# q times kᵀv for two heads: two 64-row halves of the TensorE array in place of one block-diagonal matrix

## The chip, the cores and the metric

The kernel runs on one core of a Trainium2 chip. The metric is device time of one execution in microseconds (us). A profiled execution has a span some 1.8 us shorter than its device time. A speed ratio is the mean time of one kernel's fast runs over the mean of the other's in the same rounds on the same chip, so it is not quite the ratio of the medians quoted beside it.

## The reference, cut to what matters

```python
def _attn_ref(q, k, v, g_norm):                      # 8 batches, 8 heads, 576 tokens, 64 wide, fp32
    kv = np.einsum('bhsd,bhse->bhde', k, v)
    out = np.einsum('bhsd,bhde->bhse', q, kv)
    rms = np.sqrt(np.mean(out * out, axis=-1, keepdims=True) + 1e-06)
    return (out / rms * g_norm).astype(np.float32)
def _moe_ref(x, w_gate, w_val, w_out):               # x: 4608 tokens x 512
    gate = 1.0 / (1.0 + np.exp(-(x @ w_gate)))
    val = x @ w_val
    return (gate * val @ w_out).astype(np.float32)
```

## The kernel before

Attention is done for two heads at a time, 32 pairs in all. A pair's work is a list of small steps. The first eight pairs are scheduled by hand at the start, while weights are still being converted on VectorE. The other 24 go, one step per "slot", between the matmuls of the feed-forward layers.

```python
    kvs = [const.tile([P, P], FP32, name=f"kv{i}") for i in range(2)]
    # ... zeroed once: the two off-diagonal blocks stay zero
        def kv_mm():                  # k^T v: head e on its half of the array's columns
            d["kv"] = ps = at_ps()
            for j in range(NJ):
                js = slice(HD * j, HD * j + HD)
                for e in range(2):
                    nc.tensor.matmul(ps[HD * e:HD * e + HD, 0, 0:HD], pairs[n]["k"][:, e, js], pairs[n]["v"][:, e, js],
                                     start=(j == 0), stop=(j == NJ - 1))
        def kv_out():                 # the two 64x64 blocks onto the diagonal
            for e in range(2):
                es = slice(HD * e, HD * e + HD)
                nc.vector.tensor_copy(out=kvs[n % 2][es, es], in_=d["kv"][es, 0, 0:HD])
            load_kv(n + 2)
        # ... q_mm, q_out: q is transposed, both heads' 64 rows on 128 partitions
        def u_mm():                   # q (k^T v): 96 tokens of both heads at a time
            ps = at_ps()
            d["u"] = ps[0:NP, :, 0:JH * P]
            for j in range(NJ):
                c0 = P * (j % JH)
                nc.tensor.matmul(ps[0:NP, j // JH, c0:c0 + P], d["qT"][:, j // JH, NP * (j % JH):NP * (j % JH) + NP],
                                 kvs[n % 2], start=True, stop=True)
        # ... u_square (ScalarE), u_sum (VectorE), u_root (ScalarE), u_norm (VectorE), x_mm (transposes), x_out
        return [kv_mm, kv_out, q_mm, q_out, u_mm, u_square, u_sum, u_root, u_norm, x_mm, x_out]
```

Here `P` is 128, `HD` 64, `NP` 96, `NJ` 6 and `JH` 3. After the first stage all attention steps share one PSUM tile of two banks ("at" in the profile); the first stage has four of them ("two").

## Time and profile before

| | before |
|---|---|
| time, median of 3 | 1215.44 us (1212.87 to 1215.98) |
| span of the profiled run | 1213.0 us |
| TensorE busy | 1172.0 us, 97% |
| VectorE busy | 473.5 us, 39% |
| to the second layer's first matmul | 220.6 us |
| from there to the first matmul of the fast first layer | 118.0 us |
| from there to the end | 874.4 us |

The last three rows cut the span at two landmarks of TensorE's own stream. The first stretch holds waits, in the other two TensorE is all but saturated. The second landmark can be read in the view of one line's instructions (first and last start are in us):

```profile
L489 PE MATMUL mm<-xT,gv x672: 379/379/483, 338.6 to 1160.2; 128*128 128x256 f32 x168
```

The first of these matmuls starts at 338.6 us, and 1213.0 - 338.6 = 874.4 us.

### The profile page before, as it was taken

The page shows a single profiled execution, that of the slowest core. Times are in us where ns is not written, and L with a number is a line of the kernel's source. Part 1 is how long each engine was busy: PE and PEld are TensorE (multiplying, and loading weights), DVE is VectorE, ACT ScalarE, POOL GpSimd, SP SyncE. Part 2 cuts the span into 40 slices and gives each one's busy share as a digit, 9 for nine tenths or more (in the row PEclk, how much of TensorE's full clock was granted, in tenths as well). Part 3 has the DMA queues.
Part 4 walks back from the last instruction along what each step waited for, and adds up shares of the span by engine and source line. Part 5 has one row for each costly group of instructions (what it writes and reads, how often), then busy time and mean ns, then how long its engine had stood idle before and what let it go on. Part 6 is the DMA issues. An engine that isn't in the chain of part 4 may idle for free.

```text
span 1213.0 us, 13391 instructions
## 1 busy us (share of the span) xinstructions
PE 1172.0 (97%) x5136; PEld 786.9 (65%) x5136; DVE 473.5 (39%) x845; ACT 308.5 (25%) x577; POOL 241.8 (20%) x342
## 2 busy tenths in 40 slices
PE   4788999999999999999999999999999999999998
PEld 4444444455478846885588648874888478748863
DVE  4667878303034412543045404540345125504430
ACT  3444121113033312431143203420334021101110
POOL 0000000100024401331044203330244015403410
PEclk9889999999999999999999999999999999999999
DMA  9544322131012101120211102110110000010000
GB/s 243 136 129 134 104 104 70 29 78 46 17 47 60 30 18 47 31 59 9 56 30 31 38 26 59 30 31 26 40 29 1 18 18 1 1 27 9 1 9 26
DMA packets 71582, 57.48 MB, mean 47 GB/s; under 512 B 40800, under 2 KB 65376, under 8 KB 71520
## 3 DMA queue, kind: packets, MB, share of 16 engines
q1 hardware_dynamic: 68992, 56.05, 17.0%
q10 hardware_dynamic: 2528, 0.59, 0.3%
q8 instruction: 41, 0.67, 0.2%
q14 instruction: 21, 0.17, 0.0%
HBM read 47.19 MB, written 9.44 MB: 47 GB/s over the span
## 4 chain that ended last, share of the span: by engine, by line
PE 93%; DVE 3%; ACT 2%; DMA 1%; issue 1%; ACTq 0%; SPq 0%; DVEq 0%
PE mm L489 42%; PE mm L321 23%; PE two L341 13%; PE two L321 7%; PE at L238 2%; PE two L238 2%; PE at L211 1%; PE at L264 1%; DVE sq L256 1%; PE at L224 1%; PE two L211 1%; DMA q<-in_q_dram 1%; ACT L251 1%; PE two L264 1%; DVE ms L247 1%; ACT sq L243 1%
## 5 line engine op out<-in xcount | busy, mean ns | idle before, releaser
L472 POOL TENSOR_TENSOR tw<-gv 128x256 f32<-128x256 f32 x168 | 120.4, 728 | 913.8 <-PE mm L489 691.5
L321 PE MATMUL mm<-wo,gv 128*128 128x512 f32 x672 | 290.5, 592 | 0.0
L489 PE MATMUL mm<-sx,tw 128*128 128x256 f32 x1008 | 234.2, 380 | 0.0
L321 PEld LDWEIGHTS mm<-wo,gv 128*128 128x128 f32 x672 | 127.3, 190 | 155.3 <-issue 155.0
L489 PEld LDWEIGHTS mm<-sx,tw 128*128 128x128 f32 x1008 | 188.8, 190 | 24.6
L341 PE MATMUL two<-xT,gv 128*128 128x512 f32 x384 | 176.7, 611 | 14.3 <-DVE gv L159 14.3
L501 DVE TENSOR_TENSOR gv<-mm,p 128x256 f32<-128x256 f32 x84 | 35.7, 425 | 321.2 <-PE mm L489 321.2
L489 PE MATMUL mm<-xT,gv 128*128 128x256 f32 x672 | 159.7, 380 | 1.2 <-ACT sg L326 1.2
L489 PEld LDWEIGHTS mm<-xT,gv 128*128 128x128 f32 x672 | 126.0, 190 | 21.2 <-issue 2.9
L341 PEld LDWEIGHTS two<-xT,gv 128*128 128x128 f32 x384 | 72.2, 195 | 98.2 <-issue 93.1
L472 POOL TENSOR_TENSOR tw<-gv,tw 128x256 f32<-128x256 f32 x168 | 126.2, 771 | 1.1
L321 PE MATMUL two<-wo,gv 128*128 128x512 f32 x192 | 84.6, 594 | 0.0
L326 ACT COPY sg<-mm 128x512 f32<-128x512 f32 x28 | 16.4, 585 | 264.5 <-PE mm L321 264.5
L510 DVE TENSOR_TENSOR gv<-mm,p 128x256 f32<-128x256 f32 x84 | 35.6, 424 | 114.3 <-PE mm L489 114.3
L489 PE MATMUL mm<-sx,gv 128*128 128x256 f32 x336 | 79.9, 381 | 0.0
L489 PE MATMUL mm<-xT,tw 128*128 128x256 f32 x336 | 79.9, 381 | 0.0
L519 ACT ACTIVATE sg<-sg 128x256 f32<-128x256 f32 x84 | 35.0, 417 | 162.9 <-DVE sg L518 161.6
L489 PEld LDWEIGHTS mm<-xT,tw 128*128 128x128 f32 x336 | 63.0, 190 | 8.5
L489 PEld LDWEIGHTS mm<-sx,gv 128*128 128x128 f32 x336 | 63.0, 190 | 8.5
L526 DVE TENSOR_TENSOR gv<-gv,sg 128x512 f32<-128x512 f32 x84 | 66.6, 832 | 0.2
L321 PEld LDWEIGHTS two<-wo,gv 128*128 128x128 f32 x192 | 35.8, 190 | 41.8 <-issue 41.6
L495 ACT COPY p<-mm 128x256 f32<-128x256 f32 x84 | 31.3, 372 | 93.5 <-PE mm L489 93.5
(67 smaller groups left out, 824.7 us busy)
## 6 DMA issues: line engine op xcount, KB each, us to landing
k<-in_k_dram SPq DMA_DIRECT2D x32, 288.0 KB, 3.5
v<-in_v_dram SPq DMA_DIRECT2D x32, 288.0 KB, 4.1
q<-in_q_dram SPq DMA_DIRECT2D x60, 144.0 KB, 3.1
st<-in_moe_w_gate_dram SPq DMA_DIRECT2D x12, 512.0 KB, 3.9
st<-in_moe_w_val_dram SPq DMA_DIRECT2D x12, 512.0 KB, 5.1
st<-in_moe_w_out_dram SPq DMA_DIRECT2D x12, 512.0 KB, 4.1
out_dram<-sg SPq DMA_DIRECT2D x24, 192.0 KB, 2.3
out_dram<-sg SPq DMA_DIRECT2D x24, 128.0 KB, 2.3
```

What stands on the lines that cost most here:

```text
L211: nc.tensor.matmul(ps[HD * e:HD * e + HD, 0, 0:HD], pairs[n]["k"][:, e, js], pairs[n]["v"][:, e, js], start=(j == 0), stop=(j == NJ - 1))
L238: nc.tensor.matmul(ps[0:NP, j // JH, c0:c0 + P], d["qT"][:, j // JH, NP * (j % JH):NP * (j % JH) + NP], kvs[n % 2], start=True, stop=True)
L264: nc.tensor.transpose(ps[:, j // JH, c0:c0 + NP], d["xn"][:, j // JH, P * (j % JH):P * (j % JH) + P], ident[0:NP, 0:NP])
L321: nc.tensor.matmul(ps[:, i], gv[c, f][:, ts], w["wo", f], start=(f == 0), stop=(f == NFT - 1))
L341: nc.tensor.matmul(self.ps[:, i], w[("wg", "wv")[i], self.f][:, m, :], xT[self.c][:, m, :], start=(m == 0), stop=(m == NMT - 1), skip_grou ...
L472: nc.gpsimd.tensor_tensor(out=tw[f, i], in0=b[in0], in1=b[in1] if isinstance(in1, tuple) else tw[f, in1], op=ALU.subtract)
L489: nc.tensor.matmul(ps, wt[:, m, :], xs[:, m, :], start=(new and m == 0), stop=(m == NK - 1), skip_group_check=True)
L495: nc.scalar.copy(out=d["p1"], in_=pa)
L501: tt(out=d["h"][:, h1], in0=pb, in1=d["p1"], op=ALU.add)
L510: tt(out=d["h"][:, h2], in0=pb, in1=d["p1"], op=ALU.add)
L519: nc.scalar.activation(out=d["sg"][:, h2], in_=d["sg"][:, h2], func=AF.Sigmoid)
L526: tt(out=d["h"], in0=d["h"], in1=d["sg"], op=ALU.mult)
```

## The change

Half of the block-diagonal matrix is zeros, and TensorE multiplies by them. The change gives each head its own 64 rows of the array, with a dense 64x64 kᵀv as the moving operand, and its own PSUM bank. Zeros are no longer streamed, the memsets go, and two copies of 64x64 become one of 128x64.

```diff
-    kvs = [const.tile([P, P], FP32, name=f"kv{i}") for i in range(2)]
+    kvs = [const.tile([P, HD], FP32, name=f"kv{i}") for i in range(2)]
-    for kv in kvs:
-        nc.vector.memset(kv, 0.0)
...
-            for e in range(2):
-                es = slice(HD * e, HD * e + HD)
-                nc.vector.tensor_copy(out=kvs[n % 2][es, es], in_=d["kv"][es, 0, 0:HD])
+            nc.vector.tensor_copy(out=kvs[n % 2], in_=d["kv"][:, 0, 0:HD])
...
-            d["u"] = ps[0:NP, :, 0:JH * P]
+            d["u"] = ps[0:NP, :, 0:NJ * HD]
             for j in range(NJ):
-                c0 = P * (j % JH)
-                nc.tensor.matmul(ps[0:NP, j // JH, c0:c0 + P], d["qT"][:, j // JH, NP * (j % JH):NP * (j % JH) + NP],
-                                 kvs[n % 2], start=True, stop=True)
+                for e in range(2):
+                    es = slice(HD * e, HD * e + HD)
+                    nc.tensor.matmul(ps[0:NP, e, HD * j:HD * j + HD],
+                                     d["qT"][es, j // JH, NP * (j % JH):NP * (j % JH) + NP], kvs[n % 2][es, :],
+                                     start=True, stop=True)
```

The square, sum and normalisation read the result by head instead of by slice, and the normalisation writes it back in the old order; the transposes after it are unchanged.

More of the change, by code (lines that the diff above doesn't have):

```diff
@@ L234, in u_mm @@
             ps = at_ps()
-            d["u"] = ps[0:NP, :, 0:JH * P]
+            d["u"] = ps[0:NP, :, 0:NJ * HD]
             for j in range(NJ):
-                c0 = P * (j % JH)
-                nc.tensor.matmul(ps[0:NP, j // JH, c0:c0 + P], d["qT"][:, j // JH, NP * (j % JH):NP * (j % JH) + NP],
-                                 kvs[n % 2], start=True, stop=True)
+                for e in range(2):
[3 more added lines that the diff above has]
+                                     start=True, stop=True)
         def u_square():
-            d["sq"] = sb.tile([NP, 2, JH * P], FP32, tag="sq", name="sq")
+            d["sq"] = sb.tile([NP, 2, NJ * HD], FP32, tag="sq", name="sq")
             nc.scalar.activation(out=d["sq"], in_=d["u"], func=AF.Square)
         def u_sum():
-            d["ms"] = sb.tile([NP, 2, 2 * JH], FP32, tag="ms", name="ms")
+            d["ms"] = sb.tile([NP, 2, NJ], FP32, tag="ms", name="ms")
             nc.vector.tensor_reduce(out=d["ms"].rearrange("p i n -> p (i n)"),
@@ L254, in u_norm @@
             nc.vector.reciprocal(d["ms"], d["ms"])
-            d["xn"] = d["sq"]
-            nc.vector.tensor_tensor(out=d["xn"].rearrange("p i (n d) -> p i n d", d=HD),
-                                    in0=d["u"].rearrange("p i (n d) -> p i n d", d=HD),
-                                    in1=d["ms"].unsqueeze(3).to_broadcast([NP, 2, 2 * JH, HD]), op=ALU.mult)
+            d["xn"] = d["sq"].rearrange("p e f -> p (e f)")
+            nc.vector.tensor_tensor(out=d["xn"].rearrange("p (j e d) -> p e j d", e=2, d=HD),
+                                    in0=d["u"].rearrange("p e (j d) -> p e j d", d=HD),
+                                    in1=d["ms"].unsqueeze(3).to_broadcast([NP, 2, NJ, HD]), op=ALU.mult)
         def x_mm():
@@ L263, in x_mm @@
                 c0 = NP * (j % JH)
-                nc.tensor.transpose(ps[:, j // JH, c0:c0 + NP], d["xn"][:, j // JH, P * (j % JH):P * (j % JH) + P],
+                nc.tensor.transpose(ps[:, j // JH, c0:c0 + NP], d["xn"][:, P * j:P * j + P],
                                     ident[0:NP, 0:NP])
```

## The prediction

> **What bounds the kernel now.** I read the page first, then the groups by line and shape, then the stretches, the chain of waits, and last the timeline of one attention pair record by record. The busy table says that TensorE is the bound:
>
> ```profile
> PE 1172.0 (97%) x5136; PEld 786.9 (65%) x5136; DVE 473.5 (39%) x845; ACT 308.5 (25%) x577; POOL 241.8 (20%) x342
> ```
>
> TensorE is busy 97% and nothing else passes 65%, so what matters is how long TensorE's own stream of matmuls takes. By stretches (columns: stretch, its length, busy time and count of PE, PEld, DVE, ACT, POOL, granted clock, DMA share, GB/s) that does not hold from the start:
>
> ```profile
> 0.00:60.00 60.00, 38.29 (x264) 27.40 (x265) 30.46 (x46) 22.57 (x36) 0.70 (x6) 0.91 0.80 191
> 60.00:120.00 60.00, 48.91 (x223) 25.91 (x222) 42.43 (x55) 26.75 (x39) 0.00 (x0) 0.89 0.44 129
> 340.00:945.00 605.00, 602.26 (x3031) 450.81 (x3030) 225.35 (x480) 181.32 (x355) 169.31 (x240) 1.00 0.13 35
> ```
>
> Until 120 us TensorE waits about a quarter of the time (60 - 38.29 and 60 - 48.91) inside a chain matmul, square, sum, root, normalise, transpose. From 340 to 945 us it waits 2.7 of 605 us: each nanosecond put into its stream is paid in full there, and a faster VectorE or ScalarE pays nothing.
>
> The change touches L238, q times k^T v, once per pair of heads, 32 pairs. The groups by shape:
>
> ```profile
> L238 PE MATMUL at<-kv,qT 128*96 128x128 f32 x240 | 29.5, 273 | 0.0
> L238 PE MATMUL two<-kv,qT 128*96 128x128 f32 x144 | 21.2, 307 | 0.0
> L211 PE MATMUL at<-v,k 96*64 96x64 f32 x480 | 18.4, 226 | 0.0
> ```
>
> Six matmuls a pair appear as 12 records (240 records over 20 pairs): an fp32 matmul is two passes, each with its own weight load. L211, k^T v, is the model for the changed line: it already runs two heads at once, each on a half of the array's columns. Their real pace is in the timeline (start, length, engine, line, shapes, count):
>
> ```profile
> 340.52 0.92 PE L211 MATMUL at<-v,k 96*64 96x64 f32 x24
> 341.37 1.99 PE L489 MATMUL mm<-sx,tw 128*128 128x256 f32 x8
> 343.20 1.89 PE L489 MATMUL mm<-xT,gv 128*128 128x256 f32 x8
> 344.93 0.66 PE L224 MATMUL at<-ident,q 96*128 96x96 f32 x6
> 345.42 3.65 PE L489 MATMUL mm<-sx,tw 128*128 128x256 f32 x16
> 348.91 1.47 PE L238 MATMUL at<-kv,qT 128*96 128x128 f32 x12
> 350.22 1.89 PE L489 MATMUL mm<-xT,tw 128*128 128x256 f32 x8
> ```
>
> Take starts, not lengths, since lengths overlap. From 348.91 to 350.22 the 12 passes of L238 hold TensorE 1.31 us, 109 ns each, with no gap before or after. A pass of L489 takes 216 ns ((344.93 - 343.20) / 8), so passes cost about 0.83 ns per column plus 2.5. L211's inner starts come in twos, 6 to 7 ns apart, one pair every 58 ns: two passes of 64 columns in the time of one (64 x 0.83 + 5), so the column halves do run together. But L211's block costs more than 12 x 58 = 0.70 us. The previous L489 pass starts at 340.21 and should have streamed until 340.43; L211's first weights are loaded only at 340.52 (0.09 lost); nothing runs ahead of that load, so it is exposed (about 0.05); after the last pass (start 341.21, streamed by 341.27) the next load is at 341.37 (0.10 lost), and that load of 128 columns is exposed too: the following eight records take 1.99 instead of 1.89 (0.10 lost). The sum is 0.70 + 0.34 = 1.04 us, and every L211 block from 340 us on has the same gaps to 1 ns. L238 and L224 have none of them. So using the array in halves has an entry and exit price of about a third of a microsecond.
>
> **What the Trainium skill says.** "TensorEngine Tiling (Array Packing)", Key Properties: changing the tiling mode drains TensorE, and different tiles can load and multiply in parallel. The trace agrees on both for column halves (0.34 us; starts 6 to 7 ns apart). "TensorE: Matmul & The Clock Gate", LDWEIGHTS: a load takes its columns over 1.2 GHz, whatever the contraction rows. The trace's single loads are 190, 163 and 138 ns for 128, 96 and 64 columns, a slope of 0.81 ns a column: it agrees, with some 85 ns of latency that overlaps. The same page, Part 3, What overlaps: loads and matmuls of different row groups overlap. No row-split matmul runs in the kernel before, so this trace cannot confirm it. The first page's Gotcha 1 wants row tiles in different PSUM banks; the change does that.
>
> **The change part by part.** The stationary operand stays a slice of qT, 96 columns, now twice with 64 rows each; the moving operand shrinks from 128 columns to 64. So 12 passes of (load 96, stream 128) become 24 of (load 96, stream 64), 12 on each half.
>
> A pass now streams for 64 x 0.83 = 53 ns, but the weights behind it need 96 x 0.83 = 80 ns, plus 2.5. Before, an 80 ns load hid under a 107 ns stream. Now it does not: a half has one load in flight beside its running pass, so it steps at about 85 ns (82.5 plus the 2.5 by which L211's 58 also exceeds 53 + 2.5). That a load longer than the pass above it is paid is seen after L224: its last transpose covers 82 ns of a 128-column load of 110 ns, and the 16 records after it take 3.65 us against 16 x 0.216 + 0.163 = 3.62, about the missing 28 ns.
>
> The block then costs, if the two halves load and stream together: entry drain 0.093, first load exposed 0.082, 11 steps of 0.085 = 0.935, last stream 0.058, exit drain 0.094, next load exposed 0.104. Sum 1.366 us against 1.312: plus 0.054 us. Half the multiplications by zero are gone, and the weight loads and two drains eat it.
>
> Of the 32 blocks, 24 (the 20 "at" and 4 "two" after 120 us) lie in a saturated TensorE: 24 x 0.054 = +1.3 us.
>
> The first eight lie in the chain before 120 us. It runs through the end of L238, not through what TensorE does after it, so the exit costs are off it: 1.312 becomes 0.093 + 0.082 + 0.935 + 0.058 = 1.168, minus 0.14 us, for five blocks: -0.7. The first three run wholly or partly at half clock. The chain has them so:
>
> ```profile
> 17.21 2.57 PE two L238 x12
> 19.81 0.81 ACT sq L243
> 20.63 1.28 ACT L251
> 21.93 0.31 ACT ms L251
> 22.26 0.23 DVE ms L254
> 22.55 0.04 issue
> 22.59 0.96 DVE sq L256
> ```
>
> 2.57 is 12 x 0.213. With everything doubled the new block ends after about 0.18 + 0.16 + 11 x 0.165 + 0.107 = 2.26: -0.3 twice and, estimated, -0.2 once: -0.8.
>
> VectorE: 64 copies of 64x64 (218 to 220 ns) become 32 of 128x64; a copy's time follows the 64 elements a partition, so about 32 x 0.22 = 7 us leave VectorE. None of that is on the chain: it goes from matmul to matmul past the copies. The two memsets (0.3 us together) end long before VectorE's first work at 7.3 us. L243, L247 and L256 keep 96x768; the write of L256 becomes runs of 64 at stride 128 and I expect its 953 ns unchanged. Transposes and everything after are the same work.
>
> Total: +1.3 - 0.7 - 0.8 = -0.2 us, so 1215.2; I say 1215.
>
> **Rivals.** First, halves that load and stream together with the load hidden, or twice as fast with 64 rows. Steps are then 58 ns, the block 1.07 us, and the saving 0.24 x 32 = 8 us: 1207. For it: L211 does step at 58, but there load and stream are both 53, so it cannot tell which of them binds. Against: the slope by columns. I give it 15%.
>
> Second, no drain between row halves and the whole array. The block would be about 0.082 + 0.935 + 0.058 = 1.08 plus little: again some 7 us, 1207. Against it are L211's two gaps, the same in all later blocks. 13%.
>
> Third, the two halves' weights come over one path, one load after the other. Steps are 165 ns, the block 0.093 + 0.165 + 11 x 0.165 + 0.058 + 0.198 = 2.33 us, plus 1.0 us on each of 32 blocks: 1248. For it: [...]no trace here shows row halves. Against: the skill's row overlap, and the halves are different partitions. 12%.
>
> Fourth, that VectorE's 7 us shows. It would need a VectorE-bound stretch; its fullest, 60 to 120 us, is 42.43 of 60. Under 1 us in any case.
>
> **Range and chances.** The main path (60%) lands within 3 us of 1215; the first two rivals share 28% at about 1207, the third 12% at 1248. Runs of before spread over 3 us. 1206 to 1222 covers the main path and most of the two gains. Faster by over 2% means under 1191, 24 of the 42 us that all 32 blocks cost (32 x 1.31), which no way above gives: 1%. Slower by over 2% is over 1239.7, nearly only the third rival: 10%.
>
> **What would show it.** The block at L238 measured from starts: 1.37 us with steps of 85 ns for two passes (58 is the first rival, 165 the third); starts of the two heads' passes 6 to 7 ns apart; the next load 0.09 to 0.10 us after the last stream and the following eight L489 records 1.99 instead of 1.89 us (absent in the second rival). The copy should be x32 at about 220 ns, L256 still about 953 ns. I am wrong if the row halves do not overlap, if a drain for row halves has another price, or if a new wait stands ahead of the square or the transposes.

## The result, and the profile after

The changed kernel ran in 1213.29 us (median of 4, 1211.31 to 1214.59) against 1215.49 us. The ratio is 0.9985 with a 95% interval of 0.9965 to 1.0005: the same time. The prediction was 1215.

The busy table of the changed kernel:

```profile
PE 1174.9 (97%) x5520; PEld 779.5 (64%) x5520; DVE 465.6 (38%) x811; ACT 309.0 (25%) x577; POOL 242.1 (20%) x342
```

TensorE has 384 more records (32 pairs times 12) and shows 2.9 us more busy time; VectorE lost 7.9 us. The groups by shape, for the changed matmuls and the copy:

```profile
L236 PE MATMUL at<-kv,qT 64*96 64x64 f32 x480 | 24.7, 249 | 0.0
L236 PE MATMUL two<-kv,qT 64*96 64x64 f32 x288 | 17.7, 279 | 0.0
...
L213 DVE COPY kv<-at 128x64 f32<-128x64 f32 x20 | 4.3, 217 | 1.8 <-PE at L209 1.8
```

The group's busy time fell from 29.5 to 24.7 us, and read alone it says that 4.8 us were won. It is the wrong number. The price of the drains lies outside it, in the time between the last matmul before and the first after. The timeline of TensorE around one pair (start, length, engine, line, shapes, count) shows it:

```profile
347.27 0.59 PE L489 MATMUL mm<-sx,tw 128*128 128x256 f32 x2
347.79 1.24 PE L236 MATMUL at<-kv,qT 64*96 64x64 f32 x24
348.96 1.99 PE L489 MATMUL mm<-xT,tw 128*128 128x256 f32 x8
350.79 0.38 PE L489 MATMUL mm<-sx,gv 128*128 128x256 f32 x1
```

The two passes from 347.27 stream for 0.216 us each, until 347.70; the block's first load comes 0.09 later. Its 24 passes start over 0.990 us, in twos 6 to 7 ns apart: the second two 133 ns after the first, then one pair every 85 ns. The next load stands at 348.96, 0.175 after the last start; and those eight records take 1.99 us instead of 1.89, because nothing was loaded ahead. The block costs 0.093 + 0.990 + 0.175 + 0.104 = 1.362 us, where the old one cost 1.312. All 20 later blocks show these four numbers to 1 or 2 ns.

The second landmark of the changed kernel, in the same view as before the change:

```profile
L489 PE MATMUL mm<-xT,gv x672: 379/379/483, 337.4 to 1160.0; 128*128 128x256 f32 x168
```

So the changed kernel was 1.2 us ahead here (337.4 against 338.6) and gave 1.0 back until the end: 1212.8 - 337.4 = 875.4 us. With three profiles of the changed kernel and two of the one before, the three stretches are:

| stretch, us | before (2 profiles) | after (3 profiles) |
|---|---|---|
| to the second layer's first matmul | 220.63, 218.16 | 219.22, 221.02, 222.59 |
| to the first matmul of the fast first layer | 117.97, 117.97 | 118.17, 118.17, 118.17 |
| to the end | 874.39, 874.39 | 875.41, 875.40, 875.39 |

The two later stretches repeat to 0.02 us, so 0.05 us per block can be read there without any statistics: + 0.20 for 4 blocks and + 1.01 for 20. The first stretch varies by several us from run to run of the same kernel. Taking the rest as constant in unprofiled runs as well, each timed run gives it too: its span less the constant.

### The profile page after: what moved, and what is told of

The parts are those of the page before. It is cut to its first block, busy times and chain, and to the rows that moved or that the text cites. A ratio compares the mean times of both kernels' runs of the same rounds, so it can differ in the third digit from the quotient of the medians.

```text
span 1212.8 us, 14140 instructions
## 1 busy us (share of the span) xinstructions
PE 1174.9 (97%) x5520; PEld 779.5 (64%) x5520; DVE 465.6 (38%) x811; ACT 309.0 (25%) x577; POOL 242.1 (20%) x342
## 4 chain that ended last, share of the span: by engine, by line
PE 92%; DVE 3%; ACT 2%; DMA 1%; issue 1%; SPq 0%; DVEq 0%; ACTq 0%
PE mm L489 42%; PE mm L321 23%; PE two L341 13%; PE two L321 7%; PE at L236 2%; PE at L209 1%; PE at L264 1%; PE two L236 1%; PE at L220 1%; DMA q<-in_q_dram 1%; DVE sq L256 1%; DMA v<-in_v_dram 1%; PE two L209 1%; PE two L264 1%; ACT L250 1%
```

## The experiments

All twelve runs below gave the reference's result.

### The same two kernels again

The first repeats the kernel before, the next two the changed one, without any edit.

> The kernel before, unchanged, for a second profile and the noise. Theory (the shorter chain through the new block before 120 us wins what the drains cost later): 1215 us, and the ninth block of q times k^T v, the first in the saturated part, starts at 230.8 us as in the first profile, within 0.3 us (after the change it started at 229.5). Rival (the 1.3 us by which the changed kernel was ahead there came from a different granted clock before 120 us, where three k^T v blocks ran at half clock before and one after): the start moves by 1 us or more from profile to profile of the same kernel.

> The changed kernel again, with more rounds. Theory: ratio to before 0.9985 with an interval that may just leave 1; the ninth block starts at 229.5 us within 0.3; each saturated block costs 1.362 us (from starts) against 1.312. Rival of the clock: the ninth block starts up to 1 us or more elsewhere, and the ratio is 1.000 to 1.001 when it starts late.

> The changed kernel once more, beside the one with the halves late, for the stage up to the second layer. Theory (the chain before 120 us is shorter by about 1.5 us with row halves): the time of the core less the 993.6 us of the later stretches is about 218.5 on average, 1.5 under that of the halves-late kernel. Rival (the clock's phases decide that stage and row halves change nothing): the two averages within 0.5 us.

The kernel before took 1213.43 us (ratio to itself 0.9993, 0.9969 to 1.0017). The changed kernel took 1213.74 (0.9994, 0.9974 to 1.0013) and 1215.33 (1.0006, 0.9987 to 1.0025). The mean of all 37 runs of before is 1214.0, that of the 16 of the changed kernel 1214.1: no difference.

The expectation about the ninth block failed for the reason that its rival named. It started at 230.8 and 228.3 us in the two profiles of before, and at 229.5, 231.3 and 232.8 in the three of the changed kernel. The being ahead by 1.2 us in the first pair of profiles was chance.

From block five on, what differs is TensorE's clock. A kᵀv block's 24 starts take 0.697 us at full clock and about 1.235 at half. In the hand-scheduled stage some of these blocks run at half clock, not the same ones in every profile, and the time from one q times kᵀv block to the next takes one of about three values. Matched by that pattern, though, the shorter chain shows. In steps from block five on, 14.78, 16.38 and 14.84 us (before) stand against 14.64, 16.26 and 14.71 (after, second profile); and, in runs at full clock, 13.23 and 13.29 (the block-diagonal early stage of the kernel with late halves below) against 13.10 and 13.16 (after, first profile). That is 0.12 to 0.14 us a step.

### Each half of the change alone

Row halves for the first eight pairs only, and row halves for the other 24 only:

```diff
+        halves = n < 2 * NHP          # in the other kernel: n >= 2 * NHP
...
+            if not halves:            # u_mm as it was, with the block-diagonal tile
```

> Row halves for the first eight pairs alone, the block-diagonal matrix for the other 24. Theory: the 24 saturated blocks are back at 1.312 us, so 24 x 0.050 = 1.2 us less than the changed kernel: 1212.1 us, ratio to before about 0.9975. Rival (a saturated block's cost is hidden or made up elsewhere): the same as the changed kernel, within 0.3 us in the profile.

> The other half of the change: the block-diagonal matrix for the first eight pairs, row halves for the other 24. Theory: the saturated part costs what it does in the changed kernel (875.4 us and 118.2 us for the two later stretches, 1.2 more than before), and the stage up to the second layer is that of the kernel before, whose 22 timed runs give 220.0 on average with a standard deviation of 2.4: about 1215.5, ratio to before 1.001. Rival (nothing is gained before 120 us by the row halves): the same time as the changed kernel.

With the halves early, a later block takes 1.31 us again (347.98 to 349.29, the timeline of TensorE):

```profile
347.98 1.47 PE L245 MATMUL at<-kv,qT 128*96 128x128 f32 x12
349.29 1.89 PE L511 MATMUL mm<-xT,tw 128*128 128x256 f32 x8
```

The two later stretches are 117.97 and 874.40 us, those of before; with the halves late they are 118.17 and 875.39, those of the changed kernel. So the 1.2 us are the 24 saturated blocks' and nothing hides them. The times, 1214.44 us (0.9999, 0.9981 to 1.0017) and 1215.49 us (1.001, 0.999 to 1.003), cannot show it, because the first stretch covers it up: it was 220.2 us on average in the six runs with halves early and 219.5 in the six with halves late. The expected 1212.1 was a miss. In the rounds of the halves-late kernel the changed kernel ran too (its third repeat), and there its first stretch averaged 219.7 us against 219.5: the expected 1.5 us less did not show, and the rival (within 0.5 us) held.

Over all timed runs that have a span, the spaced kernels below among them and the heads in sequence left out, the first stretch is 219.4 us with the block-diagonal matrix early (45 runs, standard error 0.4) and 218.9 with row halves early (46 runs, standard error 0.3). The 0.5 us between them have a 95% interval of about - 0.5 to + 1.4.

### Is it the weight load that sets the step?

The moving operand is made 96 columns wide in place of 64, the extra ones zero and overwritten or never read.

```diff
-    kvs = [const.tile([P, HD], FP32, name=f"kv{i}") for i in range(2)]
+    kvs = [const.tile([P, NP], FP32, name=f"kv{i}") for i in range(2)]
...
-                    nc.tensor.matmul(ps[0:NP, e, HD * j:HD * j + HD],
+                    nc.tensor.matmul(ps[0:NP, e, HD * j:HD * j + NP],
```

> The changed kernel with 96 moving columns in place of 64 (32 columns of zeros, overwritten by the next slice or never read; the result stays right). Theory (the 96-column weight load of 80 ns binds the step of 85 ns, the 53 ns stream hides under it): stream and load are now equal at 80 ns, steps stay 85 to 88 ns, only the last pass is 27 ns longer, the block 1.39 us; 32 x 0.03 = +1 us at most: about 1214.3. Rival (the step is a stream plus a fixed cost of some 32 ns for row halves): steps grow by 27 ns to 112, the block to 1.68 us, and the time by 32 x 0.32 = 10 us to about 1223.

```profile
346.57 1.26 PE L238 MATMUL at<-kv,qT 64*96 64x96 f32 x24
347.76 2.00 PE L491 MATMUL mm<-xT,tw 128*128 128x256 f32 x8
```

Half as many columns again, and the block grew from 1.17 to 1.19 us between its first start and the next group's (348.96 - 347.79, 347.76 - 346.57). Steps are still 85 ns. The last stretch is 875.94 us, 0.53 more for 20 blocks: 27 ns each, the stream of one pass that covers no load. By starts it lies between the first two pairs, 160 ns apart here and 133 in the changed kernel: a load that nothing hides, then its own stream, so the load takes about 80 ns either way (estimates from these starts: 160 - 80 and 133 - 53, with 0.83 ns a column streamed). The time was 1214.4 us (1.0009, 0.9981 to 1.0037). So the stream does not set the step. The load of 96 columns, 80 of the 85 ns, is what fits; but every run with row halves loads 96 columns, so a fixed pace of row halves, whatever is loaded, is a rival that no run here rules out.

### Do the halves overlap, and how far apart may their matmuls stand?

```diff
-            for j in range(NJ):
-                for e in range(2):
+            for e in range(2):
+                for j in range(NJ):
```

> The changed kernel with the loops swapped: six matmuls of head 0, then six of head 1, the same work in the same banks. Theory (two halves overlap only where their matmuls alternate in the stream[...]): 24 steps of 85 ns, the block 0.093 + 0.082 + 23 x 0.085 + 0.058 + 0.117 + 0.104 = 2.41 us, plus 1.05 on each block; 24 x 1.05 + 8 x about 1.0 = 33 us: about 1246. Rival (the queue reorders matmuls across the two halves, or the halves share the load path and alternate anyway): the block stays at 1.36 and the time at 1213.

```profile
354.49 1.96 PE L236 MATMUL at<-kv,qT 64*96 64x64 f32 x24
356.38 2.00 PE L489 MATMUL mm<-xT,tw 128*128 128x256 f32 x8
```

The time rose to 1234.99 us (1.0179, 1.015 to 1.0207) and the block by 0.73 us, to 1.89 between those starts against 1.17. So the overlap of the halves is worth at least that much per block, and it needs neighbours in the program. The expectation was 1.05 us a block and 1246 us: too much, because the overlap is not nil at the change of heads. One row of 12 passes starts every 85 ns until 355.475, a second row begins at 355.225 and goes on alone: three passes of the two heads run side by side where the loops have the heads in sequence.

### Is it the change of mode that costs?

The 24 later blocks are cut in two, with a slot of the main stream between.

```diff
-        return [kv_mm, kv_out, q_mm, q_out, u_mm, u_square, ...]
+        return [kv_mm, kv_out, q_mm, q_out, lambda: u_mm(0, JH), lambda: u_mm(JH, NJ), u_square, ...]
```

> The changed kernel with q times k^T v of the 24 later pairs cut into two parts of three slices, with a slot of the main stream between them: one more entry and exit per pair, the same work. Theory (an entry and an exit cost 0.093 + 0.082 + 0.117 + 0.104, against one step of 0.085 saved: about 0.37 us): the two parts together 1.73 to 1.76 us against 1.36, 24 x 0.38 = +9 us: about 1222. Rival (the gaps come from other waits, not from the change of mode): +1 us at most.

```profile
347.60 0.72 PE L236 MATMUL at<-kv,qT 64*96 64x64 f32 x12
348.25 1.99 PE L492 MATMUL mm<-xT,tw 128*128 128x256 f32 x8
350.18 0.72 PE L236 MATMUL at<-kv,qT 64*96 64x64 f32 x12
350.83 1.99 PE L492 MATMUL mm<-sx,gv 128*128 128x256 f32 x8
```

Each part has the whole price: 0.093 before it, 0.480 inside, 0.174 behind, 0.104 on the next load. That is 0.851 us, twice 1.70, and 0.34 more than one block; the slowed 1.99 stands behind both parts. The time was 1219.94 us (1.0055, 1.0017 to 1.0093). But the last stretch grew by 4.57 us, not 20 x 0.34 = 6.8. From starts, the missing 2.2 us are waits that fell away elsewhere: the transposes of the normalised result of five pairs, which fall into the second layer, came 1.07 us after the matmul before them, where 0.43 is its stream, and with one more slot ahead of them they wait no longer (- 3.2 us), while those of the other 15 pairs wait 1.1 us more in all.

Then the reverse, one entry and exit fewer. kᵀv of the next pair runs right behind q times kᵀv, into free columns of the same PSUM tile:

```diff
+            if n >= 2 * NHP and (n + 1) % NHP:          # at the end of u_mm
+                states[n + 1]["kv_mm"](ps, NJ * HD)
...
+            if n >= 2 * NHP and (n + 1) % NHP:          # at the end of u_square
+                states[n + 1]["kv_out"]()
...
+        if n > 2 * NHP and n % NHP:
+            return [q_mm, q_out, u_mm, u_square, u_sum, u_root, u_norm, x_mm, x_out]
```

> The changed kernel, but k^T v of the next pair runs right behind q times k^T v, into free columns of the same PSUM tile, for 18 of the 24 later pairs: one entry and one exit for two blocks. Theory (the tiling mode's change has a price of about 0.2 us each way, and a change from row halves to column halves costs one drain more, not two): 1.362 + 1.046 = 2.408 us becomes 0.093 + 0.990 + 0.175 + 0.697 + 0.152 + 0.104 = 2.211, so 18 x 0.197 = 3.5 us less than the changed kernel: about 1209.8 us, ratio to before about 0.9955. Rival (the gaps belong to each block whatever stands beside it): no gain, 1213.3.

```profile
350.48 1.24 PE L240 MATMUL at<-kv,qT 64*96 64x64 f32 x24
351.64 0.92 PE L213 MATMUL at<-v,k 96*64 96x64 f32 x24
352.49 1.99 PE L500 MATMUL mm<-xT,tw 128*128 128x256 f32 x8
```

The drain between the two blocks is the one exit of 0.175 us, and one entry (0.093) and one exposed load (0.104) are gone, as expected: 15 x 0.197 = 2.96 us in the last stretch. Yet that stretch was only 1.07 shorter (874.34), the stretch before it 1.0 longer (119.18), and the time 1215.13 us (0.9999, 0.9978 to 1.002). The list of waits names the new one:

```profile
PE at L224 <- ACT xT L282: 0.9, 5, 0.2
```

With kᵀv moved away, the transposes of q follow directly on the copies of x out of the one shared PSUM tile, and wait for them. From starts, the entries into q's transposes cost 1.67 us more and the transposes themselves 0.27, which with two small differences of 0.1 leaves the 1.07. The saving had turned into a wait. Where the longer stretch before it comes from was not followed here; with the waits taken away, below, it falls to 117.58.

### The waits taken away

Merged as above, with an empty slot ahead of the transposes of q and of the result; and the kernel before, with an empty slot ahead of the transposes of the result alone.

```diff
+        def empty():
+            pass
+            return [empty, q_mm, q_out, u_mm, u_square, u_sum, u_root, u_norm, empty, x_mm, x_out]   # merged
+        return [kv_mm, kv_out, q_mm, q_out, u_mm, u_square, u_sum, u_root, u_norm, empty, x_mm, x_out]
```

> As the merged kernel, with an empty slot ahead of the q transposes and ahead of the x transposes of the 24 later pairs, since the merged kernel saved 2.96 us of drains after its first-layer start but gave 1.7 us back in q transposes that waited for the copies of x. Theory (drains saved stay saved once nothing new is waited for; and the 3.2 us that TensorE waits in five x transposes in the second layer go too): from the first fast first-layer matmul to the end 870 us within 1.5, against 875.4 for the changed kernel and 874.4 before; the time about 1208, ratio to before 0.994 to 0.997. Rival (the saving moves to another wait again): 874 us or more for that stretch, the time 1213.

> The kernel before, with one empty slot ahead of the x transposes of the 24 later pairs: tells how much of the spaced kernel's gain has nothing to do with row halves or drains. Theory: the five x transposes that come in the second layer no longer wait 0.64 us each, so the stretch from the first fast first-layer matmul to the end falls from 874.4 by 2 to 3.5 us to about 871.5, the time to about 1212. Rival (the wait moves on to the transposes in the first layer): 874 us, no change.

The groups of these transposes by shape, of the kernel before, of the spaced kernel before, and of the merged and spaced one (busy, mean ns, idle before):

```profile
L264 PE MATMUL at<-ident,sq 96*128 96x96 f32 x120 | 13.6, 249 | 2.7 <-DVE sq L256 2.4
```

```profile
L264 PE MATMUL at<-ident,sq 96*128 96x96 f32 x120 | 13.2, 246 | 0.0
```

```profile
L272 PE MATMUL at<-ident,sq 96*128 96x96 f32 x120 | 13.2, 245 | 0.0
```

The 2.7 us of idle time are gone. That line shows less than was won, since a matmul's modelled length (379 ns for a pass of 256 columns) reaches beyond its streaming (216 ns) and covers part of the wait; by starts the waits fell by 5.6 us, and the last stretch by 5.57, to 868.82. The spaced kernel before ran in 1206.25 us, ratio 0.9937 (0.9916 to 0.9958). The merged and spaced one has 866.87 us in that stretch, 8.53 less than the changed kernel: 5.57 for the waits and 2.96 for the drains, so all of the drains' price stayed saved this time. It ran in 1204.72 us, ratio 0.9925 (0.9906 to 0.9943), and beats both kernels. Both gains are clear of the noise, though under 2%, and larger than expected (871.5 and 870 us for that stretch), because the transposes of the 15 pairs in the first layer had waited as well. Between the two spaced kernels, the two later stretches differ by 1.95 + 0.39 = 2.3 us; their times differ by 1.5 and the intervals overlap, so that difference is shown by the profile alone.

### VectorE's part alone

```diff
-            nc.vector.tensor_copy(out=kvs[n % 2], in_=d["kv"][:, 0, 0:HD])
+            for e in range(2):
+                es = slice(HD * e, HD * e + HD)
+                nc.vector.tensor_copy(out=kvs[n % 2][es, :], in_=d["kv"][es, 0, 0:HD])
```

> The changed kernel with the single 128x64 copy of k^T v undone: two 64x64 copies as before, so VectorE gets its 7 us back. Theory (VectorE is off the path): within 0.5 us of the changed kernel, 1213.3, VectorE busy 472 us again. Rival (the copies were the gain before 120 us, where they stand on the way from k^T v to q times k^T v): eight copies of 0.22 us come back there, up to 1.8 us: 1215.

VectorE was busy 473.2 us again. The later stretches were 118.17 and 875.37 us, those of the changed kernel, so the copies cost nothing there. The time was 1215.2 us (1.0017, 0.9988 to 1.0046). The first stretch averaged 220.0 us in four runs, against 218.7 in 16 of the changed kernel with a standard deviation of 1.9: whether the copies cost something there is inconclusive.

### What could not be tried

Both heads in one PSUM bank, with the old layout, was not run: two row halves write the same bank unordered. So whether two banks are needed is left open here; it rests on the page that the prediction cites.

## Why the prediction was right

**The block.** The predicted sum was 1.366 us, the measured one 1.362: entry 0.093, steps of 85 ns, exit and exposed load as in the model line. The pace was taken from starts rather than from busy time or mean lengths. The model was the line that already used the array in halves, with its gaps. And the load was compared with the pass that covers it. Splitting and merging show the entry and exit; the wide moving operand shows that the stream does not bind, with the rival left that is named there. One reading was too wide: the slope of 0.81 ns a column, and the page's rule that the prediction finds confirmed by it, fit the loads of matmuls. The transposes' loads of 128 columns (96 rows) took 140 ns in the same trace, not 190, and followed each other every 82 to 83 ns.

**The saturated blocks.** + 1.3 us was predicted, + 1.21 measured (0.20 + 1.01), in every profile.

**The chain before 120 us.** Here the prediction was - 0.7 for five blocks and - 0.8 for the first three. For the five, 0.12 to 0.14 a step is seen where clock patterns match, against the predicted 0.14. For the first three the step failed. "With everything doubled" had the block at 2.26 us instead of 2.57. It is shorter even than that, as the chain of waits of the changed kernel shows, for a block at half clock and one at full. But the same chain no longer runs through the first block: it comes from a load of q for the third pair, issued at 14.37 and landed at 23.96 us:

```profile
14.37 9.59 DMA q<-in_q_dram
...
24.09 1.19 PE two L220 x6
...
26.25 2.14 PE two L236 x24
...
39.82 1.19 PE two L236 x24
```

So the stage did not get shorter by it. From the first to the fourth block's start it took 20.1 to 22.0 us (mean 21.1) in four profiles with the block-diagonal matrix early, and 20.8 to 23.5 (mean 22.3) in nine with row halves. In all four the chain runs through the first block, as the prediction had it; in seven of the nine it runs through a load of q or v for the third pair instead, which took 8.0 to 10.8 us. TensorE sat idle ahead of the third pair's kᵀv for at most 1.0 us in the four and for 1.0 to 4.1 us in the nine, and that block ran at half clock in one of the four and in all nine. Where the chain passes it by, a shorter first block wins nothing. Why the third pair's kᵀv also starts later in the nine (20.6 to 23.4 us into the span, against 18.9 to 20.7), and whether the row halves have a part in it, stays open. What all timed runs say of the whole stage is 0.5 us won, with an interval that holds zero and ends just short of the predicted 1.5. So this term was sized too large, most likely by the 0.8 of the first three blocks. That the number came out all the same is no merit of this term: without the 0.8 the sum would have been 1216, which whole runs could not have told from 1215.

**The rivals.** The first (load hidden) fell with steps of 85 ns in place of 58. The second (no drain) fell with the gaps, and again with the split kernel. The third (one load path for both halves) fell with starts 6 to 7 ns apart; the loop order that runs the heads in turn shows what is lost when most of the overlap goes, 22 us instead of the 33 estimated there, with three of each head's twelve passes still side by side. The fourth (VectorE) shows nothing in the saturated stretches.

**Not foreseen.** Neither the prediction nor the change looked at the transposes, whose waits held 5.6 us in both kernels, several times what the change moved. The prediction read 2.7 us of waits from the busy time there, which is too low, since modelled lengths cover part of a wait.

## What to carry to other kernels

Before splitting the array to avoid zeros, put three numbers side by side: the stream saved per pass, the weight load that must still hide under it, and the drain at each end of the block. Here a stream cut from 107 to 53 ns brought the step only from 109 to 85, and two drains and two loads that nothing hides took that back. Read a saturated engine's pace from starts between two fixed landmarks in its stream, where 0.05 us per block is exact, instead of from whole runs that vary by 2 us. And when a saving disappears, look at which steps have become neighbours: here an empty slot was worth more than the arithmetic.

## What the Trainium skill lacked or had wrong

- "TensorEngine Tiling (Array Packing)", Theoretical Speedup, has up to 2x for a contraction of 64. Here two row halves cost 1.362 us a block against 1.312 for the whole array with zeros. The page does not name the weight load as a limit: with 96 columns loaded in fp32 the step was 85 ns over a stream of 64 columns and over one of 96 alike.
- The same page, Key Properties, says that a change of mode drains TensorE, but gives no price. Here it is 0.09 us on the way in and, past one more step, 0.09 on the way out (column halves 0.152 - 0.058 from the last start, row halves 0.175 - 0.085, the same with 64 and 96 moving columns), and on each side a load that nothing hides: 0.05 for 64, 0.08 for 96, 0.10 for 128 columns. From row to column halves it is one drain, 0.175 us from last start to next load.
- "TensorE: Matmul & The Clock Gate", Part 3, What overlaps, has matmuls start in strict program order. With the heads in sequence, three passes of the second head's row started beside the last three of the first's. The order of the compiled instructions isn't in the trace, so this may be the compiler's doing.
- The same page, Back-to-back issue gap, has no pace for fp32 matmuls (their passes are counted elsewhere in the skill). Here one shows as two records, each with its own load, and each takes 0.83 ns a column plus 2.5 (109 ns for 128, 216 for 256).
